# Later loads of a chunked recurrence moved to SyncE's queue, and a re-ordered first unit

## The chip, the cores and the metric

The kernel runs on one core of one Trainium2 chip. The metric is the device time of one execution in microseconds (us). A time is the median of a kernel's runs, with its lowest and highest in brackets. The same kernel moves by some 0.5% from run to run and by a little from chip to chip, so kernels are compared through the runs of the kernel before that were made on the same chip in the same rounds.

## The reference, cut to what matters

The first half is a recurrence over 768 tokens for 4 batches and 8 heads of width 40. The second half is a mixture of four two-layer networks over the 3072 tokens.

```python
for t in range(S):                         # B, H, S, D = 4, 8, 768, 40
    y[:, :, t] = einsum('bhd,bhde->bhe', rt, state)
    Sa = einsum('bhde,bhe->bhd', state, at)
    state = state * wt[:, :, None, :] - einsum('bhd,bhe->bhde', Sa, bt) \
            + einsum('bhd,bhe->bhde', vt, kt)
x = y.transpose(0, 2, 1, 3).reshape(3072, 320)
p = probs / (probs.sum(-1) + 1e-9)         # 4 networks, 320 -> 1024 -> 320
out = sum(p[:, e] * (relu(x @ w1[e]) @ w2[e]) for e in range(4))
```

## The kernel before

The tokens are cut into 12 chunks of 64; a chunk of two batches is a **unit**, so there are 24 units. For each unit the kernel solves a triangular system (tiles M, Z, Qc, QTc, QT), applies it (psat, SaT), makes the outputs (pxr, pdy) and the new state. Between these steps it places pieces of mixture work (products ph, po and p) for earlier units, so that TensorE never has to stand.

Two things matter here. The first is the tile **QT**: GpSimd copies most of it from QTc, and ScalarE copies its last quarter from the product pQ. Only then can TensorE start psat. The second is where the raw V and R of a unit three ahead are fetched: they are put on a list called `later`, and `mix` issues three or six of them behind each piece of mixture work, from **ScalarE's queue**.

```python
    def load_raw(q, names):

        moves = []
        for x in names:
            q.n["raw" + x] = t = raw[x]()
            heads = srcs[x].rearrange("b h t e -> (b h) t e")[q.b[0] * H:(q.b[1] + 1) * H, q.c * L:(q.c + 1) * L, :]
            heads = heads.rearrange("n (x two) e -> x n (two e)", two=2)
            for r in range(2):
                if x in "RV":

                    sets = ((slice(0, 8, 2), slice(r, 16, 4)), (slice(1, 8, 2), slice(3 - r, 16, 4)))
                else:
                    sets = ((slice(0, 8), slice(r, 16, 2)),)
                for n, hs in sets:
                    for y, w_ in enumerate((D + Q, 2 * D - Q)):
                        o = slice(64 * r + Q * y, 64 * r + Q * y + Q)
                        moves.append(lambda eng, out=t[o, n, 0:w_], in_=heads[:, hs, Q * y:Q * y + w_]: eng.dma_start(out=out, in_=in_))
        return moves
    # ... (cut)
    for u in range(3):
        begin(u)
    go(load_raw(units[0], "W"))
    load(units[0], "WBK")
    go(load_raw(units[0], "A"), nc.scalar)
    load(units[0], "V")
    go(load_raw(units[0], "V"), nc.scalar)
    go(load_raw(units[0], "R"))
    # ... (cut)
    def merge(q):

        Qc = sb.tile([P, H, Q], FP32, name="Qc", tag="q", bufs=2)
        QTc = sb.tile([P, H, Q], FP32, name="QTc", tag="q", bufs=2)
        tc.keep_in_program_order(nc.vector.transpose(out=dealt(Qc[:]), in_=q.Z))
        tc.keep_in_program_order(
            nc.vector.transpose(
                out=QTc[:].rearrange("p h r -> p (h r)"), in_=Qc[:].rearrange("p h c -> p (h c)"),
            )
        )
        q.QT = QTs()
        for i in range(P // Q):
            ins = nc.gpsimd.tensor_copy(out=q.QT[quarter(i), :, quarter(i % 2)], in_=QTc[quarter(i)])
            tc.keep_in_program_order(ins)
        yield

        py = big("pY")
        for h in range(H):
            for i in (1, 3):
                nc.tensor.matmul(
                    out=py[quarter(i - 1), h * Q:(h + 1) * Q], lhsT=q.F[quarter(i), h, 0:Q],
                    rhs=QTc[quarter(i), h, :], start=True, stop=True,
                )
        Y = sb.tile([P, H, Q], FP32, name="Yq")
        for i in (0, 2):
            nc.scalar.copy(out=Y[quarter(i)].rearrange("p h t -> p (h t)"), in_=py[quarter(i), 0:H * Q])
        yield

        pq = big("pQ")
        for h in range(H):
            for i in (0, 2):
                nc.tensor.matmul(
                    out=pq[quarter(i), h * Q:(h + 1) * Q], lhsT=Qc[quarter(i), h, :],
                    rhs=Y[quarter(i), h, :], start=True, stop=True,
                )
        for i in (0, 2):
            nc.scalar.copy(out=q.QT[quarter(i), :, quarter(1)], in_=by(pq[quarter(i), 0:H * Q], Q))
        yield
    # ... (cut)
        p = banks("psat")
        psa = quadrants(p, 0, BY_TOKENS, L, lambda j, s, i: (
            i ^ s, d_half(j, s), j, RH[half(i ^ s), head(j, s), :], q.QT[half(i ^ s), head(j, s), :],
        ))
        SX = SXs()
        if not q.end:
            at = (banks("pst"), 0) if q.start else (p, NJ * L)
            pst = quadrants(*at, BY_TOKENS, D, lambda j, s, i: (
                i ^ s, i, j, q.QT[half(i ^ s), head(j, s), :], RH[half(i ^ s), head(j, s), 0:D],
            ))
        SaT = sb.tile([P, NJ, 2, L], FP32, name="SaT", tag="step", bufs=3)
        for x in range(2):
            nc.scalar.copy(out=SaT[:, :, x, :], in_=psa[x])
        if not q.end:
            for x in range(2):
                for i in range(2):
                    s = i ^ x
                    nc.scalar.copy(out=of_slot(SX[half(i)], s)[:, :, 0:D], in_=pst[x][half(i)])
        yield
    # ... (cut)
    todo, last, later = [], [], []

    def begin_later(n):
        for move in later[:n]:
            tc.keep_in_program_order(move(nc.scalar))
        del later[:n]

    def mix(n):

        for piece in todo[:n]:
            piece()
            begin_later(3 if n > 1 else 6)
        del todo[:n]

    def run(gen, n=99):
        for _ in range(n):
            if next(gen, gen) is gen:
                break
    # ... (cut)
    ws = [within(units[u]) for u in range(3)]
    keep_warm(20)
    run(ws[0], 1)
    go(load_raw(units[1], "W"))
    run(ws[0], 1)
    load(units[1], "WBKV")
    run(ws[0], 1)
    go(load_raw(units[1], "AVR"))
    load_probs()
    run(ws[1], 1)
    run(ws[0], 2)
    substitute(units[0], nc.vector)
    run(ws[0], 1)
    set_pick()
    m, s = merge(units[0]), begin_step(0)
    run(m, 1)
    run(ws[0])
    go(load_raw(units[2], "W"))
    load(units[2], "WBKV")
    for e in range(2):
        load_piece()
        load_piece()
        load_w2(e)
    run(ws[1], 1)
    keep_warm(36)
    # ... (cut)
    for u in range(1, NU):
        q = units[u]
        m = s_next = w = iter(())
        if u + 1 < NU:
            m, s_next = merge(units[u + 1]), begin_step(u + 1)
        if u + 2 < NU:
            w = within(units[u + 2])

        def gap(n, pieces=None):
            at = 4 * u + n
            run(sum_ops, sums_at.get(at, 0))
            mix((1 if at in sparse else 2) if pieces is None else pieces)

        run(w, 1)
        run(w_next)
        run(s, 1)
        gap(0)

        early = u < 5
        if early:
            run(s, 1)
        run(w, 1)
        run(s)
        if u == 1:
            mixture_of_unit(q)
        elif q.bp:
            mixture_of_chunk(units[u - 1:u + 1], chunks_x[q.c])
        begin_later(len(later))
        run(w, 1)
        if not early:
            run(m, 1)
        gap(1)

        if u + 3 < NU:
            go(load_raw(begin(u + 3), "WA"))
            load(units[u + 3], "WBKV")
            later.extend(load_raw(units[u + 3], "VR"))
        run(w, 2)
        if not early:
            run(s_next, 1)
            run(m, 1)
        gap(2)

        run(m, 1)
        run(w, 1)
        if not early:
            run(s_next, 1)
        if u + 2 < NU:
            substitute(units[u + 2], nc.gpsimd)
        if early:
            run(m, 1)
            run(s_next, 1)
            run(m)
            gap(3, 1)
            run(s_next, 1)
            mix(0 if 4 * u + 3 in sparse else 1)
        else:
            gap(3)
        s, w_next = s_next, w
```

SyncE's queue issues everything else: raw W and A, the token-major tensors, the mixture's weights (w1p) and the transposed outputs (xT).

## Time and profile before

| | before |
|---|---|
| median of 3 runs at first | 1228.22 us (1220.45 to 1231.55) |
| profiled span | 1225.0 us |
| TensorE busy | 1135.7 us |
| TensorE idle before psat, with no releaser named | 43.0 us in 18 waits |
| mean granted TensorE clock | 0.958 |

The prediction below shows the lines for these. Two more of the profile's parts are needed. The first is the row of the granted clock in 40 equal slices (9 is 90% or more of full speed). The second is the list of DMA queues: packets, megabytes, and the share of the 16 engines' time.

```profile
PEclk7979999989999999999999899998899999999999
...
q1 hardware_dynamic: 224040, 110.33, 36.2%
q10 hardware_dynamic: 48400, 10.38, 4.7%
```

There are two hardware queues in use: the smaller one, with 48400 packets, is ScalarE's.

In a timeline line the columns are: start, duration, engine, source line, operation, out<-in, the operands' sizes, the number of instructions and, in brackets, the idle time just before and what ended it. A line of the table of waits gives engine, line, what it waited for, then us in total, times and the longest.

### The profile page before, as it was taken

The page shows a single profiled execution, that of the slowest core. Times are in us where ns is not written, and L with a number is a line of the kernel's source. Part 1 is how long each engine was busy: PE and PEld are TensorE (multiplying, and loading weights), DVE is VectorE, ACT ScalarE, POOL GpSimd, SP SyncE. Part 2 cuts the span into 40 slices and gives each one's busy share as a digit, 9 for nine tenths or more (in the row PEclk, how much of TensorE's full clock was granted, in tenths as well). Part 3 has the DMA queues.
Part 4 walks back from the last instruction along what each step waited for, and adds up shares of the span by engine and source line. Part 5 has one row for each costly group of instructions (what it writes and reads, how often), then busy time and mean ns, then how long its engine had stood idle before and what let it go on. Part 6 is the DMA issues. An engine that isn't in the chain of part 4 may idle for free.

```text
span 1225.0 us, 38138 instructions
## 1 busy us (share of the span) xinstructions
PE 1135.7 (93%) x16036; PEld 1002.9 (82%) x16036; DVE 757.2 (62%) x1560; ACT 335.6 (27%) x841; POOL 471.9 (39%) x1217
## 2 busy tenths in 40 slices
PE   5988999988998999899999899999899999999998
PEld 4866777777987889788889788897798888888887
DVE  7855567856747667567567476575575665744434
ACT  1312342322231332332322323323223223222110
POOL 4005466570633525426336245255163362360000
PEclk7979999989999999999999899998899999999999
DMA  6687465534344343443442443433335423222320
GB/s 103 154 216 173 84 143 126 106 74 94 81 113 106 85 111 81 105 95 88 115 106 71 106 107 92 109 91 98 91 81 132 95 69 96 73 78 73 96 82 21
DMA packets 272610, 123.14 MB, mean 101 GB/s; under 512 B 217480, under 2 KB 245816, under 8 KB 272440
## 3 DMA queue, kind: packets, MB, share of 16 engines
q1 hardware_dynamic: 224040, 110.33, 36.2%
q10 hardware_dynamic: 48400, 10.38, 4.7%
q8 instruction: 126, 2.06, 0.7%
q14 instruction: 44, 0.36, 0.1%
HBM read 112.77 MB, written 3.93 MB: 95 GB/s over the span
## 4 chain that ended last, share of the span: by engine, by line
PE 85%; DVE 6%; issue 4%; DMA 3%; ACT 1%; SPq 1%; ACTq 0%; DVEq 0%
PE ph L690 28%; PE p L797 26%; PE ph L682 9%; PE pdy L360 3%; PE psat L360 3%; PE pfe L360 2%; PE pxr L360 2%; PE prn L360 2%; PE po L731 1%; PE pc L360 1%; PE pQ L553 1%; PE pY L541 1%; DMA rawV<-in_v_dram 1%; PE pNT L324 1%; PE pev L360 1%
## 5 line engine op out<-in xcount | busy, mean ns | idle before, releaser
L690 PE MATMUL ph<-xT,w1p 128*128 128x256 f32 (+1 forms) x1520 | 352.8, 386 | 0.0
L690 PEld LDWEIGHTS ph<-xT,w1p 128*128 128x128 f32 x1520 | 280.5, 195 | 66.8 <-issue 27.0
L502 POOL TENSOR_TENSOR Z<-M,Z 128x62 f32<-128x62 f32 (+7 forms) x352 | 151.8, 431 | 457.7 <-DVE M L495 431.9
L515 POOL TENSOR_TENSOR Z<-Z 128x31 f32<-128x31 f32 (+7 forms) x704 | 245.5, 349 | 55.2
L791 DVE TENSOR_TENSOR a<-hs 128x512 f32<-128x512 f32 x220 | 154.3, 719 | 141.2 <-ACT hs L695 141.2
L695 ACT ACTIVATE hs<-ph 128x512 f32<-128x512 f32 (+1 forms) x208 | 116.6, 564 | 297.7 <-PE ph L690 296.7
L708 DVE SCALAR_TENSOR_TENSOR osb<-p,gate,osb 128x320 f32<-128x320 f32 (+1 forms) x243 | 108.3, 483 | 94.9 <-PE p L797 90.5
L797 PE MATMUL p<-sums,a 128*128 128x160 f32 x1056 | 164.8, 299 | 0.0
L797 PEld LDWEIGHTS p<-sums,a 128*128 128x128 f32 x1056 | 152.9, 190 | 2.2
L682 PE MATMUL ph<-xT,w1p 64*128 64x256 f32 (+1 forms) x760 | 119.9, 429 | 5.1 <-issue 4.1
L797 PE MATMUL p<-w,hs 128*128 128x160 f32 x704 | 102.9, 299 | 0.0
L797 PE MATMUL p<-w,a 128*128 128x160 f32 x704 | 102.8, 299 | 0.0
L797 PEld LDWEIGHTS p<-w,hs 128*128 128x128 f32 x704 | 100.2, 190 | 2.2
L797 PEld LDWEIGHTS p<-w,a 128*128 128x128 f32 x704 | 98.0, 190 | 0.0
L534 POOL COPY QT<-QTc 32x256 f32<-32x256 f32 x96 | 53.1, 553 | 109.8 <-DVE QTc L528 99.3
L682 PEld LDWEIGHTS ph<-xT,w1p 64*128 64x128 f32 x760 | 72.9, 205 | 20.3 <-issue 6.8
L479 DVE STREAM_TRANSPOSE M<-blocks 128x1024 f32<-128x1024 f32 x24 | 46.9, 1954 | 45.2 <-ACT blocks L476 44.7
L360 PE MATMUL psat<-QT,RH 64*64 64x64 f32 x704 | 25.8, 261 | 42.3 <-issue 40.1
L360 PEld LDWEIGHTS psat<-QT,RH 64*64 64x64 f32 x704 | 20.8, 164 | 47.7 <-issue 46.6
L371 DVE COPY_PREDICATED ET<-mask_up,pfe 128x256 f32<-128x256 int32 x48 | 18.6, 439 | 62.0 <-ACT F L450 61.9
L558 ACT COPY QT<-pQ 32x256 f32<-32x256 f32 x48 | 17.4, 362 | 132.5 <-DMA rawV<-in_v_dram 77.8
L400 DVE RECIPROCAL gp<-gp 128x320 f32<-128x320 f32 x24 | 50.9, 2119 | 0.1
(135 smaller groups left out, 1410.7 us busy)
## 6 DMA issues: line engine op xcount, KB each, us to landing
w1p<-in_moe_w_dram SPq DMA_DIRECT2D x95, 512.0 KB
w1p<-in_moe_w_dram SPq DMA_DIRECT2D x190, 64.0 KB
w<-in_moe_w_dram SPq DMA_DIRECT2D x4, 1280.0 KB
sums<-in_moe_w_dram SPq DMA_DIRECT2D x9, 512.0 KB
natW<-in_w_dram SPq DMA_DIRECT2D x48, 80.0 KB
natB<-in_b_dram SPq DMA_DIRECT2D x48, 80.0 KB
natK<-in_k_dram SPq DMA_DIRECT2D x48, 80.0 KB
natV<-in_v_dram SPq DMA_DIRECT2D x48, 80.0 KB
```

Of the source, the lines that this page charges most:

```text
L360: nc.tensor.matmul(out=p[row][half(col), lo + at * out_cols:lo + (at + 1) * out_cols], lhsT=lhsT, rhs=rhs, start=(n == 0), stop=(n == len( ...
L400: nc.vector.reciprocal(out=gp[:], in_=gp[:])
L479: ins = nc.vector.transpose(out=M[:], in_=cols)
L502: ins = eng.tensor_tensor(out=Z[:, 1:3, 0:n, j + 1:Q], in0=M[:, j:j + 2, None, j + 1:Q].to_broadcast([P, 2, n, m]), in1=Z[:, here, 0:n, j: ...
L515: eng.tensor_tensor(out=z[:, 0], in0=z[:, 0], in1=z[:, x], op=ALU.add)
L534: ins = nc.gpsimd.tensor_copy(out=q.QT[quarter(i), :, quarter(i % 2)], in_=QTc[quarter(i)])
L682: nc.tensor.matmul(out=ph[i][:, f, :], lhsT=w1.last[i * DT:(i + 1) * DT, f, :], rhs=xT[i * DT:(i + 1) * DT, 2, :], start=(f == 0), stop=False,
L690: nc.tensor.matmul(out=ph[i][:, f, :], lhsT=w1.main[:, g, at * P:(at + 1) * P], rhs=xT[:, g, :], start=False, stop=(g == 1 and f == HF // ...
L695: nc.scalar.activation(out=h[:, i * HF // 2:(i + 1) * HF // 2, 0:n], in_=ph[i][:], func=ACTF.Relu,)
L708: nc.vector.scalar_tensor_tensor(out=to, in0=p, scalar=sc, in1=to, op0=ALU.mult, op1=ALU.add)
L791: nc.vector.tensor_tensor(out=t[:], in0=x, in1=y, op=op)
L797: nc.tensor.matmul(out=p[:, n * HD:(n + 1) * HD], lhsT=a[:, f, :], rhs=b[:, f, :], start=(f == 0), stop=(f == HF - 1),)
```

## The change

The intent is to free ScalarE's queue of the loads, so that its copies start when their input is there, and to shorten the first unit's chain. There are three parts: all later V and R transfers are issued from SyncE; R and V of units 0 and 1 are fetched token-major and turned by TensorE, not VectorE; VectorE's instructions of the first unit are pinned in program order. The core of the diff:

```diff
+    def load_padded(q, x):
+        t, moves = padded[x, q.u], []
+        for i, bb in enumerate(q.b):
+            for n, h in ((0, 0), (1, 1), (2, 3), (3, 2)):
+                src = srcs[x][bb, h::4, q.c * L:(q.c + 1) * L, :].rearrange("h t e -> t h e")
+                moves.append(lambda eng, out=t[part(i), n::4, 0:D], in_=src: eng.dma_start(out=out, in_=in_))
+        return moves
 ...
-            if q.u == 1 or also:
+            if q.u < 2 or also:
                 tc.keep_in_program_order(ins)
 ...
-        turn_raw(VT[:], n["rawV"][:])
-        turn_raw(q.RT[:], n["rawR"][:])
+        def turn_padded():
+            for x, t in (("R", q.RT), ("V", VT)):
+                nc.scalar.copy(
+                    out=t[:].rearrange("p (i j) t -> p j i t", i=2),
+                    in_=turn(f"p{x}T", tok(padded[x, q.u]))[:].rearrange("p (j i t) -> p j i t", i=2, t=L),
+                )
+        if q.u == 1:
+            turn_padded()
+        elif q.u > 1:
+            turn_raw(VT[:], n["rawV"][:])
+            turn_raw(q.RT[:], n["rawR"][:])
 ...
     def begin_later(n):
         for move in later[:n]:
-            tc.keep_in_program_order(move(nc.scalar))
+            tc.keep_in_program_order(move(nc.sync))
         del later[:n]
 ... (cut: the new order of loads, warming products and steps of units 0 to 2)
```

More of the change, by code (lines that the diff above doesn't have):

```diff
@@ L92 @@
     mask_up = const.tile([P, L], I32, name="mask_up")
-    nc.vector.tensor_copy(out=mask_up[:], in_=upf[:])
     def dealt(x):
@@ L100 @@
     unit_cols = const.tile([P, Q // 4, Q], FP32, name="unit_cols")
-    nc.vector.transpose(out=unit_cols[:], in_=dealt(diagf[:, None, :].to_broadcast([P, H, Q])))
     PLACES = [(g, j) for g in range(3) for j in range(NJ) if 2 * j * D < (g + 1) * P and 2 * (j + 1) * D > g * P]
@@ L148 @@
     of_64 = [P, H, 64]
+    padded = {}
+    for n, (x, u) in enumerate((x, u) for u in range(2) for x in "RV"):
+        t = padded[x, u] = sums[n // 2][:, n % 2 * H * 64:(n % 2 + 1) * H * 64].rearrange("p (h e) -> p h e", e=64)
+        nc.gpsimd.memset(t[:, :, D:64], 0.0)
     raw = {x: kept(f"raw{x}", [P, 2 * NJ, 2 * D], 1, 0.0, nc.vector, D + D - Q) for x in "WARV"}
@@ L202, in load_raw, with part @@
         return moves
+    def load_padded(q, x):
[5 more added lines that the diff above has]
+        return moves
+    def part(i):
+        return slice(i * L, (i + 1) * L)
     def go(moves, eng=None):
@@ L216 @@
         begin(u)
+    tc.keep_in_program_order(nc.vector.tensor_copy(out=mask_up[:], in_=upf[:]))
+    ins = nc.vector.transpose(out=unit_cols[:], in_=dealt(diagf[:, None, :].to_broadcast([P, H, Q])))
+    tc.keep_in_program_order(ins)
     go(load_raw(units[0], "W"))
@@ L219 @@
     go(load_raw(units[0], "A"), nc.scalar)
-    load(units[0], "V")
-    go(load_raw(units[0], "V"), nc.scalar)
-    go(load_raw(units[0], "R"))
+    go(load_padded(units[0], "R"), nc.scalar)
     w2_sb = [const.tile([P, NF, DM], FP32, name=f"w2_{e}") for e in range(E)]
@@ L306, in quarter @@
         return slice(Q * q, Q * q + Q)
-    def part(i):
-        return slice(i * L, (i + 1) * L)
     def of_slot(x, s):
@@ L394, in within @@
         nc.vector.tensor_tensor(out=q.gl[:], in0=q.gl[:], in1=Gv[:, :, L - 1:L], op=ALU.mult)
+        q.AT = sb.tile([P, 2 * NJ, L], FP32, name="AT", tag="AT", bufs=2)
+        if q.u == 0:
+            pin(turn_raw(q.AT[:], n["rawA"][:]))
         yield
@@ L399, in within @@
         pin(nc.vector.tensor_tensor(out=gp[:], in0=pg, in1=n["W"][:], op=ALU.mult))
-        nc.vector.reciprocal(out=gp[:], in_=gp[:])
+        pin(nc.vector.reciprocal(out=gp[:], in_=gp[:]))
         yield
@@ L415, in within @@
         q.K, q.N = k_tok(), n_tok()
-        nc.vector.scalar_tensor_tensor(
+        ins = nc.vector.scalar_tensor_tensor(
             out=q.N[:, :, 0:D], in0=n["B"][:], scalar=-1.0, in1=gp[:], op0=ALU.mult, op1=ALU.mult,
         )
-        nc.vector.tensor_tensor(out=q.K[:, :, 0:D], in0=n["K"][:], in1=gp[:], op=ALU.mult)
-        q.AT = sb.tile([P, 2 * NJ, L], FP32, name="AT", tag="AT", bufs=2)
-        turn_raw(q.AT[:], n["rawA"][:])
+        pin(ins)
+        pin(nc.vector.tensor_tensor(out=q.K[:, :, 0:D], in0=n["K"][:], in1=gp[:], op=ALU.mult))
+        if q.u > 0:
+            pin(turn_raw(q.AT[:], n["rawA"][:]))
         at_ij = q.AT[:].rearrange("p (i j) t -> p i j t", i=2)
-        nc.vector.tensor_tensor(out=at_ij, in0=at_ij, in1=Gv.rearrange("p (j i) t -> p i j t", i=2), op=ALU.mult)
+        ins = nc.vector.tensor_tensor(out=at_ij, in0=at_ij, in1=Gv.rearrange("p (j i) t -> p i j t", i=2), op=ALU.mult)
+        pin(ins)
         q.VC = VCs()
@@ L467, in within @@
         if q.u == 0:
+            turn_padded()
             causal_scores()
@@ L893 @@
     ws = [within(units[u]) for u in range(3)]
-    keep_warm(20)
+    keep_warm(16)
     run(ws[0], 1)
     go(load_raw(units[1], "W"))
-    run(ws[0], 1)
+    go(load_padded(units[0], "V"))
+    load(units[0], "V")
+    run(ws[0], 2)
+    run(ws[1], 1)
+    go(load_padded(units[1], "R"))
     load(units[1], "WBKV")
-    run(ws[0], 1)
-    go(load_raw(units[1], "AVR"))
+    go(load_raw(units[1], "A"))
     load_probs()
-    run(ws[1], 1)
     run(ws[0], 2)
@@ L909 @@
     run(ws[0])
+    for move in load_padded(units[1], "V"):
+        tc.keep_in_program_order(move(nc.scalar))
     go(load_raw(units[2], "W"))
     load(units[2], "WBKV")
+    run(ws[1], 1)
+    keep_warm(36)
+    run(ws[1], 1)
     for e in range(2):
@@ L915 @@
         load_w2(e)
-    run(ws[1], 1)
-    keep_warm(36)
-    run(ws[1], 1)
     go(load_raw(units[2], "AVR"))
```

## The prediction

> **What bounds the kernel now.** I read the busy table and the chain that ended last first, to learn which engine sets the time:
>
> ```profile
> PE 1135.7 (93%) x16036; PEld 1002.9 (82%) x16036; DVE 757.2 (62%) x1560; ACT 335.6 (27%) x841; POOL 471.9 (39%) x1217
> PE 85%; DVE 6%; issue 4%; DMA 3%; ACT 1%; SPq 1%; ACTq 0%; DVEq 0%
> ```
>
> TensorE is the bound: 85% of the chain, and idle for only 1225.0 - 1135.7 = 89 us. A gain must come out of those 89 us or out of a lowered clock (0.958 granted on average). So I asked who TensorE waits for, and then who ScalarE (ACT) waits for:
>
> ```profile
> PE psat L360 <- issue: 43.0, 18, 5.6
> PE pNT L324 <- DVE n_tok L416: 7.3, 4, 4.2
> ACT QT L558 <- DMA rawV<-in_v_dram: 77.8, 11, 9.0
> ACT QT L558 <- DMA rawA<-in_a_dram: 20.3, 2, 10.6
> ```
>
> Half of the idle time stands before one product, psat, in 18 of the 24 units, and the view names no releaser ("issue"). But psat reads QT, and ScalarE's copy that fills QT is what starts late, after DMA issues. The timeline of one unit shows it, three engines side by side (start us, us, engine, line, operation; idle before it in brackets):
>
> ```profile
> 391.65 0.69 PE L553 MATMUL pQ<-Yq,Qc 32*32 32x32 f32 x32
> 392.79 0.65 PE L360 MATMUL pfe<-AT,KT 64*64 64x64 f32 x32
> 399.02 1.45 PE L360 MATMUL psat<-QT,RH 64*64 64x64 f32 x30 [5.58 <-issue]
> ...
> 391.39 7.13 ACTq L201 DMA_DIRECT2D rawV<-in_v_dram  x6
> 398.56 0.75 ACT L558 COPY QT<-pQ 32x256 f32<-32x256 f32 x2 [10.55 <-DMA rawA<-in_a_dram]
> ...
> 393.15 2.87 SPq L267 DMA_DIRECT2D w1p<-in_moe_w_dram  x3
> 396.75 2.49 SPq L201 DMA_DIRECT2D rawA<-in_a_dram  x4
> ```
>
> pQ is done at 392.3. The copy pQ->QT takes 0.75 us, yet starts at 398.56: from 391.39 ScalarE's queue is issuing six rawV transfers, which took 7.13 us instead of 6 x 0.47. The built program shows why: each transfer waits for an earlier one on its completion semaphore (eight are shared by both issuing engines), so ScalarE waits for SyncE's transfers of that moment. TensorE stands 5.58 us. I read this as the cause in nearly all 18.
>
> The stage table gives the size (stretch: us, busy of PE, PEld, DVE, ACT, POOL, granted clock, DMA share, GB/s):
>
> ```profile
> 300.00:1023.30 723.30, 681.88 (x10020) 609.96 (x10021) 464.00 (x945) 210.65 (x527) 311.88 (x795) 0.96 0.41 97
> 200.00:300.00 100.00, 88.16 (x1316) 74.73 (x1308) 72.35 (x138) 28.16 (x73) 44.55 (x109) 0.91 0.46 103
> ```
>
> From 300 to 1023 us TensorE is idle 723.3 - 681.9 = 41.4 us, and the waits of that stretch put 41.1 of it before psat.
>
> **What the Trainium skill says.** "PSUM — Partial Sum Buffer", section "Engine vs sequencer instructions": ScalarE's queue is strict first-in-first-out. The trace agrees: the QT copy stands behind the issues for 6.2 us though its input is ready. "DMA: Bandwidth & Descriptors", section "Issuing engines are not separate DMA queues": transfers from any engine run on the same 16 DMA engines, and issuing from several saves only sequencer time. So the move should cost only SyncE's time; 0.41 DMA share in the steady stretch leaves room. Same page, "Queues, rings and completion order": each DMA engine round-robins between queue rows. Moving V and R behind the weights on one row takes that turn-taking away; no run has shown yet what this costs. "TensorE: Matmul & The Clock Gate", Part 1: an idle window of about 3.4 us halves the clock. Here smaller gaps already show it: after the 3.76 us wait at 683 us the 16 ph products at 691 took 4.80 us instead of 3.65.
>
> **The change, part by part.** (a) *Later V and R transfers from ScalarE to SyncE.* Removed from ScalarE: 869 - 556 = 313 rows of the built queue; 320 issues x 0.47 us = 150 us plus their waits. ScalarE is not the bound, so only what passes to TensorE counts. After it, QT is copied at about 392.4 and ready at 393.2, while pfe ends at 393.4: the psat wait should shrink from 2.4 us to a few tenths.
>
>  - Idle removed, 300 to 1023 us: about 41 us.
>  - Clock: in 10 us stretches of that stage the granted clock dips after most stalls (0.82 to 0.84, and 0.66 twice); the deficits add up to about 25 us. About 60% of such a stretch is work, so 15 us. A cross-check: between psat at 300.45 and psat at 1023.33 lie 15 units, 48.2 us each. Units with the stall subtracted and a clock of 1.00 take 44.1 to 44.6. (48.2 - 44.35) x 15 = 58 us against 41 + 15 = 56.
>  - 200 to 300 us: idle 11.8 us and clock 0.91. Only the ScalarE-made share goes: I choose 8 us idle and 3 us clock. 140 to 200: 2 us.
>
> (b) *R and V of units 0 and 1 turned on TensorE.* Four VectorE transposes of 0.71 us go (2.8 us); four groups of four TensorE transposes (0.6 us warm, 1.1 cold each) and four ScalarE copies of about 0.6 us come. The built order puts them after pev and after the 36 warming products, where TensorE only waits or warms: nothing on the path. The number of transfers stays the same (8 in place of 8 for each tensor and unit).
>
> (c) *VectorE's order pinned.* Before, gp waited behind AT and the VT transpose (12.01 against pg ready at 11.15): 0.8 us. Unit 1's G work (0.45 + 0.45 + 0.16 + 0.07 + 1.22 + 0.17 = 2.5 us) lay inside unit 0's substitution, which is on the chain until 37.7 us; the built order puts it ahead, into a VectorE gap of 3.1 us. As it overlapped partly, I count 1.6 us. Together 2.4 us, and unit 1's n_tok comes 2.4 us earlier, which opens SyncE's queue for the first weights (at 47.1 before). From there to about 95 us the stage is limited by transfers (217 GB/s from 61 to 92), so those 2.4 us just move through.
>
> Sum: 56 + 11 + 2 + 2.4 = 71 us. New small waits I put at 0.6 us for each of 17 steady units, 10 us. Gain 61 us, from 1228.2: **1168 us** after rounding up.
>
> **Rivals.** *SyncE's queue becomes the new wait.* It gets about 16 x 0.47 = 7.5 us of issues a unit. Its load in a unit is then about: small tensors 5, raw W and A 4, V and R 7.5, four weight pieces 6, xT 6, stores 1: 30 of 44 us. Against this rival:
>
> ```profile
> SPq L267 <- PE ph L690: 263.0, 52, 9.2
> ```
>
> The queue stands 263 us waiting for TensorE to free a weight buffer, so it has time. I walked one unit through the new order: the tightest weight piece, behind the twelve xT transfers, still lands about 7 us before its use; xT itself is used only three gaps (30 us) later, since six pieces of mixture work are waiting. If I am wrong, TensorE waits on w1p 2 us a unit: 1205 us.
>
> *V and R land later, behind a 640 KB piece in the same row.* R's last four would land about 3 us later. In the old VectorE order RT stood ahead of n_tok, with 1.7 us to spare before pNT; the built order moved RT behind k_tok, which defuses it, but then QTc and pY have only about 2 us. If it bites: 1 to 2 us a unit, 1185 to 1200 us.
>
> *The psat wait has another cause* (QT's GpSimd copies, RH): against this, GpSimd ends its QT copies at 382.0 and RH is made at 385.6, both long before 393. If the stall merely shrank by half: 1198 us. *Only the idle goes and the clock stays:* 1185 us.
>
> **Range and chances.** The mechanism is seen directly in one unit and counted in 18; the size is checked twice; the built order shows no new wait on ScalarE. All rivals leave a gain. I say 1168, with 1150 to 1192 for 8 in 10; at 1204 the gain would be 2%. Faster 0.94, same 0.05, slower 0.01.
>
> **What would show it.** Right: psat's wait on TensorE falls from 43 us to under 8; ScalarE's QT copies no longer name rawV; granted clock near 0.985; psat to psat about 45 us; unit 0's QTc about 2 us earlier. Wrong: waits of ph on w1p or xT, of pY on QTc, or of pNT on n_tok in most units; or psat still waiting with ScalarE free of transfers.

## The result, and the profile after

| | before | after |
|---|---|---|
| median, with lowest and highest | 1229.59 us (1220.45 to 1231.55), 4 runs | 1164.72 us (1162.15 to 1168.46), 4 runs |
| profiled span | 1225.0 us | 1166.6 us |
| granted clock of the profiled run | 0.958 | 0.966 |

The ratio of the two is 0.9482, with a 95% interval of 0.943 to 0.9534. A ratio here is the mean time of one kernel's runs over that of the other's runs of the same rounds, so it is not quite the ratio of the medians. The changed kernel is faster, and correct. The profile was taken in the slowest of its four runs.

The busy table, the clock row, the queues and the chain that ended last, after:

```profile
PE 1119.5 (96%) x16044; PEld 993.8 (85%) x16044; DVE 758.5 (65%) x1556; ACT 334.0 (29%) x845; POOL 472.9 (41%) x1221
...
PEclk7888898899999999999999999999999999999999
...
q1 hardware_dynamic: 268968, 119.78, 42.3%
q10 hardware_dynamic: 3472, 0.62, 0.3%
...
PE 85%; SPq 4%; DVE 3%; DMA 3%; issue 2%; POOL 2%; ACT 1%; ACTq 0%; DVEq 0%; POOLq 0%
```

TensorE's idle time fell from 89 to 47 us. Its busy time fell by 16 us as well, though it has 8 more instructions: it ran at a higher clock. The clock row has no dip left after the first quarter. The move shows in the queues: 44928 packets went from the small one to the large one.

The waits of the changed kernel:

```profile
PE pY L571 <- DVE QTc L558: 5.6, 4, 2.2
...
PE psat L373 <- issue: 2.1, 1, 2.1
...
ACT QT L588 <- PE pQ L583: 76.2, 21, 4.4
...
SPq L283 <- PE ph L720: 156.4, 41, 9.8
```

The wait before psat went from 43.0 us to 2.1 us. ScalarE's QT copy now waits for pQ, its real input, in 21 units, and no longer names a transfer. SyncE's queue, with the added issues, still stands 156 us waiting for TensorE to free a weight buffer, so it has room. One unit of the steady stage, the same as the prediction showed:

```profile
386.86 0.69 PE L583 MATMUL pQ<-Yq,Qc 32*32 32x32 f32 x32
387.48 0.69 PE L373 MATMUL pfe<-NT,AT 64*64 64x64 f32 x32
387.60 0.75 ACT L588 COPY QT<-pQ 32x256 f32<-32x256 f32 x2 [4.38 <-PE pQ L583]
388.00 0.65 PE L373 MATMUL pfe<-AT,KT 64*64 64x64 f32 x32
388.46 0.68 PE L373 MATMUL psat<-QT,RH 64*64 64x64 f32 x31
```

The QT copy starts 0.05 us after pQ ends, runs beside pfe, and psat follows pfe with no gap. From the psat of the unit at 300.4 us before (301.2 after) to that of the unit at 1023.3 us before (965.2 after), the 15 units take 722.9 us before and 664.0 us after: 48.2 and 44.3 us each. The stage gained 59 us, as much as the whole kernel did (58.4 us in the profiled spans).

So what happened in the first 300 us, where 13 us more had been expected? The stage table of both kernels, before and then after (columns as in the prediction: stretch, busy of PE, PEld, DVE, ACT and POOL, granted clock, DMA share, GB/s):

```profile
140.00:300.00 160.00, 145.97 (x2394) 121.78 (x2394) 113.21 (x218) 50.57 (x136) 85.57 (x212) 0.95 0.50 110
```
```profile
140.00:300.00 160.00, 149.78 (x2458) 126.07 (x2460) 113.60 (x217) 52.27 (x140) 89.64 (x217) 0.94 0.40 89
300.00:970.00 670.00, 664.79 (x10186) 598.62 (x10180) 471.97 (x960) 211.01 (x538) 310.20 (x795) 0.99 0.45 107
```

In the steady stage TensorE is busy 664.8 of 670 us at a clock of 0.99. Between 140 and 300 us it is still idle for 10 us, and the clock is no better than before. Following psat unit by unit, the changed kernel is 3.9 us behind at unit 2 (144.5 against 140.6 us), 14 us behind at unit 3 (187.2 against 173.0) and level again at unit 6 (301.2 against 300.4).

In the start, the timeline of before and then of after:

```profile
29.25 9.08 PE L890 MATMUL warm<-ident 128*128 128x128 f32 x72
...
37.73 0.45 DVE L528 STREAM_TRANSPOSE QTc<-Qc 128x256 f32<-128x256 f32 x1
38.32 0.69 PE L541 MATMUL pY<-QTc,F 32*32 32x32 f32 x32
```
```profile
22.89 1.09 PE L373 MATMUL pev<-VC,ET 64*64 64x40 f32 x32 [5.86 <-ACT VC L486]
...
28.52 10.01 PE L920 MATMUL warm<-ident 128*128 128x128 f32 x72
34.10 0.45 DVE L558 STREAM_TRANSPOSE QTc<-Qc 128x256 f32<-128x256 f32 x1
38.36 0.60 PE L337 MATMUL pRT<-ident,sums 128*128 128x128 f32 x4
39.33 0.69 PE L571 MATMUL pY<-QTc,F 32*32 32x32 f32 x32
```

QTc does come 3.6 us earlier, but pY, which reads it, starts 1.0 us later: the warming products and unit 1's turn pRT (and pVT behind it) stand ahead of it in TensorE's order and end at 39 us. Here TensorE's own order had taken the place of VectorE as the limit.

### The profile page after: what moved, and what is told of

Read it like the earlier page. It is cut to its first block, busy times and chain, and to the rows that moved or that the text cites.

```text
span 1166.6 us, 38288 instructions
## 1 busy us (share of the span) xinstructions
PE 1119.5 (96%) x16044; PEld 993.8 (85%) x16044; DVE 758.5 (65%) x1556; ACT 334.0 (29%) x845; POOL 472.9 (41%) x1221
## 4 chain that ended last, share of the span: by engine, by line
PE 85%; SPq 4%; DVE 3%; DMA 3%; issue 2%; POOL 2%; ACT 1%; ACTq 0%; DVEq 0%; POOLq 0%
PE ph L720 29%; PE p L827 28%; PE ph L712 9%; PE pdy L373 3%; PE psat L373 2%; PE pxr L373 2%; PE prn L373 2%; SPq L204 2%; PE pfe L373 2%; PE po L761 1%; PE pc L373 1%; POOL Z L545 1%; PE pQ L583 1%; PE pY L571 1%; PE pev L373 1%
## 5 line engine op out<-in xcount | busy, mean ns | idle before, releaser
L532 POOL TENSOR_TENSOR Z<-M,Z 128x62 f32<-128x62 f32 (+7 forms) x352 | 143.1, 406 | 375.6 <-DVE M L525 349.7
L545 POOL TENSOR_TENSOR Z<-Z 128x31 f32<-128x31 f32 (+7 forms) x704 | 258.2, 367 | 55.2
L712 PE MATMUL ph<-xT,w1p 64*128 64x256 f32 (+1 forms) x760 | 111.3, 402 | 2.3 <-issue 2.3
L564 POOL COPY QT<-QTc 32x256 f32<-32x256 f32 x96 | 49.8, 519 | 132.4 <-DVE QTc L558 127.3
L712 PEld LDWEIGHTS ph<-xT,w1p 64*128 64x128 f32 x760 | 68.4, 190 | 16.0 <-issue 6.1
L373 PE MATMUL pdy<-VC,k_tok 64*64 64x104 f32 (+1 forms) x768 | 43.2, 266 | 0.0
L493 ACT COPY EV<-pev 64x160 f32<-64x160 f32 x96 | 23.4, 286 | 64.0 <-PE pev L373 63.5
L444 ACT COPY VC<-natV 128x320 f32<-128x320 f32 x23 | 10.6, 459 | 107.9 <-PE pdy L373 98.9
L373 PE MATMUL pdy<-SX,n_tok 64*64 64x104 f32 (+1 forms) x768 | 40.5, 253 | 0.4 <-DVE SX L384 0.4
```

Source lines behind the costliest of these rows:

```text
L373: nc.tensor.matmul(out=p[row][half(col), lo + at * out_cols:lo + (at + 1) * out_cols], lhsT=lhsT, rhs=rhs, start=(n == 0), stop=(n == len( ...
L532: ins = eng.tensor_tensor(out=Z[:, 1:3, 0:n, j + 1:Q], in0=M[:, j:j + 2, None, j + 1:Q].to_broadcast([P, 2, n, m]), in1=Z[:, here, 0:n, j: ...
L545: eng.tensor_tensor(out=z[:, 0], in0=z[:, 0], in1=z[:, x], op=ALU.add)
L712: nc.tensor.matmul(out=ph[i][:, f, :], lhsT=w1.last[i * DT:(i + 1) * DT, f, :], rhs=xT[i * DT:(i + 1) * DT, 2, :], start=(f == 0), stop=False,
```

## The experiments

Twelve kernels ran, in three batches; each batch has its own runs of the kernel before on the same chip. All gave a correct result. Times are medians.

| run | time, us | ratio to before (95%) |
|---|---|---|
| first batch: before | 1227.37 (1223.51 to 1230.66) | |
| e1: only the queue | 1163.09 (1161.0 to 1167.46) | 0.948 (0.945 to 0.9509) |
| e2: only the start | 1221.48 (1220.47 to 1222.58) | 0.9952 (0.9925 to 0.998) |
| e3: V on ScalarE | 1243.26 (1237.35 to 1249.12) | 1.0128 (1.0085 to 1.0171) |
| e4: R on ScalarE | 1170.68 (1162.71 to 1172.91) | 0.9525 (0.9484 to 0.9566) |
| second batch: before | 1226.99 (1222.07 to 1231.67) | |
| e5: both on ScalarE, behind the QT copy | 1181.89 (1180.34 to 1184.13) | 0.9631 (0.9594 to 0.9668) |
| e6: unit 3's substitution on VectorE | 1166.06 (1165.41 to 1167.55) | 0.9502 (0.9467 to 0.9537) |
| e7: 12 warming products | 1164.97 (1161.4 to 1168.29) | 0.9501 (0.9457 to 0.9544) |
| e8: units 2 and 3 on VectorE | 1166.01 (1163.95 to 1169.07) | 0.9502 (0.9464 to 0.954) |
| third batch: before | 1233.93 (1230.24 to 1236.88) | |
| e9: the changed kernel again | 1163.8 (1161.96 to 1165.84) | 0.9435 (0.9411 to 0.946) |
| e10: units 4 and 5 on ScalarE, behind QT | 1145.65 (1142.81 to 1151.25) | 0.9296 (0.9268 to 0.9323) |
| e11: e10 with 12 warming products | 1147.85 (1142.49 to 1150.13) | 0.9302 (0.9275 to 0.9328) |
| e12: units 4 to 7 on ScalarE, behind QT | 1157.5 (1154.93 to 1159.12) | 0.9382 (0.9357 to 0.9406) |

The theory: nearly the whole gain comes from the queue of the later transfers, because six V issues stood in ScalarE's queue ahead of the QT copy. The rivals: the start brings a good part of it; or any load on ScalarE's queue costs the same, wherever it stands.

### e1 and e2: each part alone

e1 is the kernel before with one word changed; e2 is the changed kernel with that word changed back.

```diff
 e1, from the kernel before                          e2, from the changed kernel
-  tc.keep_in_program_order(move(nc.scalar))         -  tc.keep_in_program_order(move(nc.sync))
+  tc.keep_in_program_order(move(nc.sync))           +  tc.keep_in_program_order(move(nc.scalar))
```

> The kernel before with one word changed: the later V and R transfers go to SyncE's queue; the start is the old one. Theory (the queue alone makes the gain, in the steady stage; the new start gives nothing or costs a few us): 1158 to 1168 us, psat's wait on TensorE under 6 us, from psat at 300 us to the one fifteen units later 665 us instead of 723. Rival (the new start is needed, it carries a quarter or more of the 65 us): 1180 us or more.

> The changed kernel with one word put back: later transfers on ScalarE's queue again, the new start kept. Theory: 1225 to 1238 us, psat's wait back at 40 us or more, granted clock back near 0.96. Rival (the new start carries a part of the gain): 1215 us or less.

e1 took 1163.09 us, a ratio of 0.948 where the whole change has 0.9482. The queue alone is the gain. Its steady stage is that of the changed kernel:

```profile
300.00:970.00 670.00, 665.57 (x10227) 601.51 (x10222) 474.93 (x963) 211.35 (x540) 312.64 (x804) 1.00 0.44 108
```

e2 took 1221.48 us, just under its expected range. Its waits are those of before, and the QT copy names the transfers again:

```profile
PE psat L373 <- issue: 38.4, 16, 4.9
...
ACT QT L588 <- DMA rawV<-in_v_dram: 55.0, 8, 9.8
ACT QT L588 <- DMA rawA<-in_a_dram: 34.3, 4, 9.2
```

So the new start is worth 0.5% beside the old queue, and nothing that can be seen beside the new one. Why the two parts don't add up was not tested.

### e3 and e4: V alone or R alone on ScalarE

In the built order, six V transfers stand directly ahead of each QT copy, and no R transfer does. So V on ScalarE should bring the stall back, and R should not.

```diff
-            later.extend(load_raw(units[u + 3], "VR"))
+            for x, eng in (("V", nc.scalar), ("R", nc.sync)):      # e4: V on sync, R on scalar
+                later.extend((eng, move) for move in load_raw(units[u + 3], x))
```

> The changed kernel with only V's later transfers on ScalarE, R's on SyncE. In the built order the six V issues then stand just ahead of the copy that fills QT. Theory (what counts is issues ahead of that copy, not transfers on ScalarE as such): nearly the whole loss comes back, 1205 to 1235 us, psat's wait 30 us or more. Rival (each transfer on ScalarE costs its share, half the transfers half the loss): 1195 us.

> The mirror image: only R's later transfers on ScalarE, V's on SyncE. No issue stands ahead of the QT copy; R's eight stand ahead of the EV and RS copies and of later ones. Theory: 1160 to 1172 us, psat's wait under 6 us, as in the changed kernel. Rival (half the transfers half the loss): 1195 us.

e4 took 1170.68 us, as expected: with eight transfers a unit on ScalarE, but none ahead of QT, nearly all of the gain is there. e3 took 1243.26 us: slower than the kernel before, and above its expected range. Its waits, and the stall at one unit:

```profile
PE psat L373 <- issue: 55.0, 16, 5.9
...
ACT QT L588 <- DMA rawA<-in_a_dram: 63.5, 7, 10.7
```
```profile
389.81 6.56 ACTq L204 DMA_DIRECT2D rawV<-in_v_dram  x6
394.15 3.68 SPq L204 DMA_DIRECT2D rawA<-in_a_dram  x4
396.41 0.75 ACT L588 COPY QT<-pQ 32x256 f32<-32x256 f32 x2 [8.07 <-DMA rawA<-in_a_dram]
```

ScalarE's six issues end at 396.37, and the copy starts at once. In the steady stage (blocks that start between 300 and 1030 us) a block of six V issues takes 5.5 us in the kernel before (mean of 15 blocks) and in e2 (15 blocks), and 7.3 us in e3 (14 blocks), against an estimated 2.8 us for six issues of the 0.47 us that the prediction counted. In e3 SyncE's queue has R's transfers as well. The timeline shows a block as one row. The packed trace has its six issues one by one, each with the semaphore that it waits for and the times of that semaphore's updates, and with them the wait can be read. Before the second to sixth issues of a block, ScalarE's queue stands 42 us in all in the kernel before and 72 us in e3 (stops over 0.25 us). Each of these stops ends within 0.2 us of an update of the semaphore that the issue waits for, and the transfer that was issued on this semaphore last was always one of SyncE's (w1p, raw W, and natK or natB, the token-major K and B). So the block's extra time is waiting for SyncE's transfers, as the prediction had read from the built program.

### e5: all on ScalarE again, but behind the QT copy

This separates the queue from the place in it. The list is held back from where it is filled until psat has been issued.

```diff
     def begin_later(n):
+        if hold:
+            return
         for move in later[:n]:
-            tc.keep_in_program_order(move(nc.sync))
+            tc.keep_in_program_order(move(nc.scalar))
 ...
             later.extend(load_raw(units[u + 3], "VR"))
+            hold.append(u)
 ... behind the step that issues psat, in both branches:
+            hold.clear()
+            begin_later(6)
```

> The changed kernel with all later V and R transfers back on ScalarE's queue, but none of them ahead of the QT copy of a unit: the first six are issued directly behind psat's copies. Theory (the place ahead of the QT copy did the harm, not ScalarE's queue as such): psat's unnamed wait stays under 8 us, granted clock at least 0.96, time 1160 to 1190 us. Some cost may be left where the six now stand ahead of the copies of the substitution. Rival (any issues on ScalarE's queue hold up its copies, wherever they stand): psat or another product waits 20 us or more and the time is 1200 us or above.

It took 1181.89 us, inside the theory's range: 74% of the gain comes back with ScalarE's queue as it was and only the place changed ((1 - 0.9631) / (1 - 0.9501), with e7 as the full gain of that batch, since the changed kernel itself did not run in it). This share is that of the whole time, with an early lead in it that is told below; a unit of the steady stage alone gets back 2.3 of the 3.8 us, some 60% (from the pY of unit 8 to that of unit 22: 48.1 us a unit before, 45.8 in e5, 44.3 in the changed kernel). The psat wait is 6.0 us. The rest turned into another wait, which these lines of e5 show, first the steady stage's waits, then one unit:

```profile
PE pY L571 <- DVE QTc L558: 13.6, 7, 2.9
...
ACT blocks L506 <- DMA rawV<-in_v_dram: 25.4, 8, 4.6
...
DVE M L509 <- ACT blocks L506: 69.8, 15, 7.0
```
```profile
385.94 1.29 ACTq L204 DMA_DIRECT2D rawV<-in_v_dram  x3
387.26 0.81 ACT L506 COPY blocks<-F 32x256 f32<-32x256 f32 x2 [1.68 <-DMA rawA<-in_a_dram]
```

The six issues now stand ahead of ScalarE's copies into `blocks`. These copies start the chain of M (VectorE), Z (GpSimd), QTc (VectorE) and pY (TensorE). VectorE's M waits 69.8 us for `blocks` in the steady stage against 24.5 us in the changed kernel, and TensorE's pY waits 13.6 us where it has none in the changed kernel (all its four waits of pY lie before 300 us). A unit takes 45.8 us against 44.3 (from the pY of unit 8 to that of unit 22).

One thing had not been expected: up to 300 us e5 was ahead of the changed kernel. Its psat of unit 6 comes at 290.5 us, against 301.2 us. This is where the missing 13 us had to be looked for.

### e6 and e8: is it GpSimd's substitution?

In the changed kernel the chain that ended last runs through a substitution on GpSimd (tile Z) between 188 and 211 us. The first theory for the early loss was therefore that this substitution bounds the stage, and it was taken for that of unit 3. In e6 and e8 VectorE does unit 3's substitution instead: from 140 to 165 us GpSimd is busy for 1.7 us in place of 18.4.

```diff
-            substitute(units[u + 2], nc.gpsimd)
+            substitute(units[u + 2], nc.vector if u == 1 else nc.gpsimd)
 ... and in e8 also, ahead of the loop:
-    substitute(units[2], nc.gpsimd)
+    substitute(units[2], nc.vector)
```

> The changed kernel with the forward substitution of unit 3 on VectorE instead of GpSimd. Theory (between 150 and 215 us the chain runs through GpSimd's substitution of unit 3, and that is where the expected gain of the first 300 us went): psat of the unit at 301 us comes 3 to 8 us earlier and the total falls by as much, 1157 to 1163 us. Rival (TensorE has other work to fill that time, which it does later anyway): total within 2 us of the changed kernel.

> As the run with unit 3's substitution on VectorE, with unit 2's there too. Theory: 0 to 4 us below that run if unit 2's chain also bounds; rival: VectorE, which has 71 us of work in the 100 us from 140 on, gets crowded, and the total is the same or up to 5 us above it.

They took 1166.06 and 1166.01 us: no gain. The psat of unit 6 comes at 303.0 and 302.7 us, no earlier than the 301.2 of the changed kernel. But the edit missed its target. Unit 3's pY starts at 182.3 us in the changed kernel, so the substitution from 188 us on cannot be unit 3's: it is that of unit 4, and ends just before unit 4's pY (212.9). Unit 3's ran from 145 to 167 us, where the chain goes through TensorE. In e6 the chain still runs through unit 4's substitution on GpSimd:

```profile
189.65 0.98 POOL Z L532
...
214.50 1.06 PE pY L571 x32
```

So the two runs show that moving the substitutions of units 2 and 3 gains nothing. Whether unit 4's, which is on the chain, costs time stays untested.

### e7: fewer warming products

```diff
-    keep_warm(36)
+    keep_warm(12)
```

> The changed kernel with 12 instead of 36 warming products in front of the turns of unit 1. Theory (the 36 products, 10.0 us up to 38.5 us, and the turns hold back pY, which had its input at 34.6): pY of unit 0 starts 2 to 4 us earlier, at 35.5 to 37; as transfers bound the stage up to 95 us, the total moves by 0 to 3 us. Rival (a colder clock takes it back): pY earlier but its products and the ones up to 60 us slower, total the same or worse.

The timeline of the start:

```profile
27.06 4.99 PE L920 MATMUL warm<-ident 128*128 128x128 f32 x24
...
34.19 0.69 PE L571 MATMUL pY<-QTc,F 32*32 32x32 f32 x32 [1.26 <-DVE QTc L558]
```

pY comes 5.1 us earlier, and now waits for QTc, its input. So the warming products and the turns behind them did hold it back. The total is 1164.97 us: nothing is gained that the spread of 7 us would let one see. The changed kernel did not run in this batch; e11 below repeats the test with its control beside it.

### e9 to e12: the early stretch

The built orders of TensorE show what the early stretch hangs on. Ahead of unit 3's pY stand 216 products of the mixture (ph and po, as the program has them) in the kernel before, in e2 and in e5, and 252 in the changed kernel, e1, e6, e7 and e8. Ahead of units 4 and 5 they differ by 1 and 4 products, and from unit 6 on they are the same. The move to SyncE's queue, which lies behind this, made the scheduler put 36 products ahead of unit 3's chain. e4 and e3, with 233 and 244, stand between, and the step from unit 2's psat to unit 3's follows the count: 32.4 us before, 32.6 in e2 and 34.1 in e5 with 216 products, 35.4 in e4, 38.4 in e3, 42.7 in the changed kernel and in e1 with 252.

In e10 only the later transfers of units 4 and 5 go back to ScalarE, held behind the QT copy as in e5; that brings the 216 back. e12 does so for units 4 to 7. e11 is e10 with 12 warming products, and e9 the control.

```diff
-            later.extend(load_raw(units[u + 3], "VR"))
+            early_on_act = u <= 2                                   # e12: u <= 4
+            later.extend((nc.scalar if early_on_act else nc.sync, move) for move in load_raw(units[u + 3], "VR"))
+            hold.extend([u] if early_on_act else [])
 ... behind psat in the branch of the early units:
+            if hold:
+                hold.clear()
+                begin_later(6)
```

> The changed kernel again, as the control of this batch: 1161 to 1168 us.

> The changed kernel, with the later V and R transfers of units 4 and 5 alone on ScalarE's queue, none of them ahead of a QT copy; all others stay on SyncE. In the built order this puts 216 instead of 252 products of the mixture ahead of unit 3's pY on TensorE, as the kernel before has it. Theory (the gain that was expected between 140 and 300 us is lost because the move to SyncE's queue made the scheduler put 36 products of the mixture ahead of unit 3's chain): psat of the unit at 301 us comes 7 to 12 us earlier, and the total is 6 to 12 us below the control, 1152 to 1159 us. Rival (the mixture work put ahead is done anyway and its time comes back later): within 3 us of the control.

> The run before with 12 instead of 36 warming products at 28 us. Theory (the products hold back the first pY by 5 us, and this lead is kept to the end): 3 to 7 us below the run before. Rival (the stage up to 95 us is bound by transfers, so the lead is lost there): within 2 us of the run before.

> As the run with units 4 and 5, but units 4 to 7 on ScalarE behind the QT copy. Theory (behind the QT copy ScalarE's queue still costs 1.5 to 2 us a unit, as the period of 45.9 against 44.4 us says): 3 to 4 us slower than the run with two units. Rival (the cost belongs to later units alone): the same.

e9 repeated the changed kernel: 1163.8 us. e10 took 1145.65 us, 18 us less and well apart in the intervals: more than the 6 to 12 us expected, and the fastest kernel. TensorE's order ahead of unit 3's pY, in e9:

```profile
164.58 4.47 PE L761 MATMUL po<-w,hs 128*128 128x320 f32 x16
...
174.97 1.78 PE L761 MATMUL po<-w,hs 128*128 128x320 f32 x6
176.68 0.69 PE L373 MATMUL pc<-RT,VT 40*64 40x64 f32 x32
...
179.99 0.69 PE L571 MATMUL pY<-QTc,F 32*32 32x32 f32 x32 [0.95 <-DVE QTc L558]
```

and in e10, with the stage table of the two stretches below it:

```profile
156.42 0.69 PE L373 MATMUL pc<-RT,VT 40*64 40x64 f32 x32
...
160.31 0.69 PE L373 MATMUL pfe<-NT,AT 64*64 64x64 f32 x32
...
161.41 0.69 PE L571 MATMUL pY<-QTc,F 32*32 32x32 f32 x32
```
```profile
140.00:300.00 160.00, 155.42 (x2559) 133.10 (x2556) 121.78 (x234) 56.78 (x152) 94.64 (x229) 0.98 0.50 116
300.00:970.00 670.00, 667.18 (x10143) 601.83 (x10142) 474.31 (x963) 207.79 (x528) 321.75 (x821) 1.00 0.44 106
```

In e9 some 12 us of mixture work run between 164.6 us and pc; in e10 pc comes ahead of most of it, and pY of unit 3 starts at 161.4 instead of 180.0 us. Between 140 and 300 us TensorE is busy 155.4 us in e10 and 149.9 in e9, at a clock of 0.98 and 0.95. psat of unit 6 comes at 279.2 us, in e9 at 298.2. Of these 19 us, 5 were there at unit 1 already (89.4 against 94.3), where the two built orders are the same, so 5 us are chance of the profiled run (e12, which has e10's order up to there, has 94.6); 14 us arose between unit 1 and unit 6, and the medians differ by 18. So the mixture work put ahead was not simply done early.

The delay shows first in the step from unit 2's psat to unit 3's: 42.2 us in e9 and 35.1 in e10. The units after it, 3 to 6, take 113.2 and 107.3 us. Behind unit 3's psat TensorE in e9 is busy for 34.7 of 39 us (185 to 224 us), at a clock of 0.86 and then 0.76, and in e10 for 37.5 of 38 us (172 to 210 us) at 1.00. In e9 GpSimd's substitution of unit 4 is on the chain here as well (from 186 us), and in e10 it is not; whether it would be without the late start of unit 3 was not tested. Nor is the order alone enough for the second part: e5 and e12 have the 216 products too, and take 114.7 and 118.0 us from unit 3 to unit 6. What is also not separated is the order itself from the queue that brings it about: SyncE's queue stands 7.7 us for VectorE's VT at that point in the changed kernel, and e10 removes both.

e12 took 1157.5 us, 12 us more than e10, where 3 to 4 us were expected. Its pY of unit 3 is early (167.6 us), but from unit 4's psat (212.3 against 204.9 in e10) to unit 6's (297.3 against 279.2) it loses 11 us. Its steady stage is that of e10 (667.0 us busy of 670). So the loss belongs to two early units, not to 1.5 us for each; what causes it there was not tested.

e11 took 1147.85 us, no less than e10. Its psat of unit 0 came 3.1 us earlier (36.7 against 39.8 us), that of unit 1 only 0.4 us (89.0 against 89.4). A lead in the first unit is lost by 90 us. From 44 to 100 us the transfers run at 246 GB/s, which agrees with the rival's reason; that they are the bound there was not tested. The rival's number was right.

## Why the prediction was right or wrong

The predicted time was 1168 us and the measured one 1164.72 us, well inside the range. The mechanism of the steady stage was right; several terms of the sum were not, and they cancelled: 10 us were taken off for waits of which about half came, and of 13 us of early gain only 3 came. That the total is within 4 us is luck in this part.

- **The steady stage** (term a): 41 us of idle time and 15 us of clock, 56 together, against 59 measured. The split was a little different: between the two psats idle time fell from 41.0 to 5.2 us, by 36, and busy time from 681.9 to 658.8 us, by 23, at a clock of 0.99 in place of 0.96. The unit's period was foreseen at 44.35 us and is 44.27. e1 shows that the queue alone does this, e3 and e4 that V's transfers ahead of the QT copy do it, and e5 that their place there is some 60% of it; the rest came back where e5's issues stand ahead of another copy.
- **New small waits**, 10 us: mis-sized. TensorE is idle for only 5.2 us of 670 in that stage, and the 59 us measured already contain them.
- **200 to 300 us and 140 to 200 us**, 13 us together: this step failed. From unit 2's psat to unit 6's the changed kernel took 156.7 us against 159.8, a gain of 3.1 us. The gain is there from unit 3's psat to unit 6's (114.0 us against 127.4), but the step from unit 2 to unit 3 took 42.7 us against 32.4: the move to SyncE's queue put 36 mixture products ahead of unit 3's chain. e10 shows that more than the 13 us is to be had. e6 and e8 rule out GpSimd's substitutions of units 2 and 3 as the cause, but not that of unit 4. The prediction looked at the built order only for new waits on ScalarE and around one steady unit, not at TensorE's order in the early units.
- **"Nothing on the path"** for the turns (term b): wrong in its reasoning, harmless in its size. In the profile the turns and the warming products hold pY back until 39.3 us, though QTc was ready at 34.6. e7 and e11 show that this costs nothing in the end.
- **2.4 us of the start that "just move through"** (term c): wrong beside the new queue. QTc came 3.6 us earlier, pY 1.0 us later; e1 without the new start is as fast as the whole change. e11 shows a lead of the first unit lost by 90 us.
- **A reading**: the prediction calls its 3.76 us wait at 683 us a smaller gap than the 3.4 us that it had named. It is longer, so it shows nothing of the kind; the last section has waits that do.
- **The rivals**: SyncE's queue did not become the wait (it stands 156 us for TensorE); V and R landing later did not delay pY in the steady stage; psat's wait had no other cause; and the clock rose with the idle time gone, from 0.96 to 0.99 in the steady stage.
- **What would show it**: psat's wait (under 8 foreseen, 2.1 found), QT's releaser and the period came as written; the mean clock, 0.985 foreseen, came to 0.966, because of the first 300 us; QTc came 3.6 us earlier where 2 were foreseen.

## What to carry to other kernels

Look at which compute instruction stands directly behind a block of DMA issues on a compute engine's queue: six issues there cost about 5% here, while the same issues behind the copy that TensorE waits for cost about a quarter of that over the whole kernel and 40% of it in a steady unit, and on the queue of an engine that computes nothing they cost nothing in the steady stage. After moving transfers, compare the built order of the busiest engine unit by unit, because a scheduler may answer by moving other work: here two units' transfers put back were worth another 18 us. A piece of work that holds something up is a suspicion only: the first unit's warming products held pY up by 5 us, and taking most of them off gave nothing. And before a rival is called tested, look in the new trace whether the edit took the suspected work away: in e6 it moved the substitution of another unit.

## What the Trainium skill lacked or had wrong

- "DMA: Bandwidth & Descriptors", section "Issuing engines are not separate DMA queues", says that issuing from several engines saves only sequencer time, which is usually small. It lacks the other side: issues on a compute engine's queue hold up that engine's next instruction for longer than their own time. Six issues took 5.5 us before and 7.3 us in e3, where six times 0.47 us make an estimated 2.8 us, and having them ahead of the copy was worth most of the 5% of the kernel.
- "TensorE: Matmul & The Clock Gate", Part 1, gives an idle window of about 3.4 us for the lower clock; what a single shorter gap does it doesn't say. Here one was enough: in the kernel before, psat at 830 us waited 2.66 us, and the granted clock (the third column from the end) fell to 0.50 in the next 5 us. It is not the only one: of the psat waits before, from 300 us on, those of 1.6, 1.7, 2.2, 2.7 (twice) and 2.9 us each have a drop to 0.50 beginning within 1 us of their end, and those of 0.9, 1.3, 1.4 and, once, 2.3 us have none, so the length alone does not decide. Whether the small products just ahead of these waits (pQ and pfe) count as idle too was not tested.

```profile
830.06 1.44 PE L360 MATMUL psat<-QT,RH 64*64 64x64 f32 x30 [2.66 <-issue]
```
```profile
825.00:830.00 5.00, 2.40 (x102) 2.05 (x100) 2.04 (x4) 0.38 (x2) 0.00 (x0) 0.98 0.66 133
830.00:835.00 5.00, 4.94 (x74) 3.87 (x75) 1.34 (x5) 3.48 (x11) 0.00 (x0) 0.50 0.55 132
```

- No page that was read here says how a scheduler's order on one engine answers to a change of another engine's DMA queue; it moved 36 of TensorE's products ahead of a chain, and e10, which undoes that and puts two units' transfers back, was 18 us faster.
